# Early sums of eight rows by identity matmuls, the first weight's maxima found ahead of its conversion, and the first tile's g written in float16 directly

## The chip, the cores and the metric

The kernel runs on one core of one Trainium2 chip. The metric is the device time of one execution in microseconds (us). The engines are named as the profile names them: PE (TensorE, the matrix engine), DVE (VectorE), ACT (ScalarE), POOL (GpSimd) and SP (SyncE, which here issues every DMA). Each runs its own list of instructions in order and waits on semaphores for the others.

## The reference

Inputs q, k, v are float32 of shape (8 batches, 8 heads, 576 tokens, 64). The weights are float64: moe_w_in and moe2_w_in are 512 x 2048, moe_w_out and moe2_w_out 2048 x 512. The output is float32, 4608 x 512.

```
k_p = k.reshape(B, H, 72, 8, 64).mean(axis=3)      # means of eight rows; v the same
attn = softmax(q @ k_p.T / 8);  a = attn @ v_p     # a as 4608 tokens x 512
h = a @ moe_w_in
g = where(h >= 1, h, where(h <= -1, 0, (h + 1)**2 / 4))
x2 = g @ moe_w_out
h2 = x2 @ moe2_w_in;  out = (h2 * sigmoid(h2)) @ moe2_w_out
```

## The kernel before

Every product of the two MLPs is made of three float16 matmuls: an operand is split into a high half `hi` and a remainder `lo`, and `three` (L119 to L122) adds hi*hi, hi*lo and lo*hi in PSUM. The 4608 tokens go in nine tiles of 512. This text is about tile 0, which the kernel treats in a way of its own, and about tile 1's attention, which is laid beside it.

Early part. The sums of eight rows of k and v of batch 0 are made per pair of heads (`kv_pool`): on DVE by a reduction (L389), or for the three pairs in `ON_POOL` (v of batch 0, k and v of batch 1) on POOL by three additions (L386, L387). The attention of tile 0 goes through `att_qT`, `att_scores`, `att_norm`, `att_T` and `att_pv` in float32 and leaves tile 0's input as `xh`, `xl`.

The first weight. moe_w_in comes in nine pieces (`cuts1`: seven of 256 columns, two of 128), each loaded as pairs of int32 and converted by the six steps of `steps`: ACT takes absolute values of the high words (L174), DVE floors them and finds the piece's maximum on the way (L182), a matmul with the identity and a DVE reduction spread it to all partitions (L107, L108), three DVE operations put the number together from its two words (L95, L194, L200), ACT scales it by a power of two made from that maximum (L207) and casts it to `hi` (L212), and POOL makes `lo` (L213). The second weight, moe_w_out, goes through the same steps in eight halves, two for each of the four blocks `d` of 128 output columns.

h of tile 0. For each of 16 blocks `s` of 128 hidden columns `emit_h` issues 12 matmuls into a PSUM bank (`hps`). Then `pre_A` (ACT), `min_A` (DVE), `mid_A` (ACT) and `post_A` (DVE) compute g in float32, with constants that don't know yet how large the weight's largest element is; the 16 float32 results lie in `slots`. When the last piece is converted, `consts_A` gives the scale and `first_split` makes the two float16 halves (L808 to L815), one block by ACT and DVE, the next by ACT and POOL.

y of tile 0. For each `d` in turn the two halves of moe_w_out are converted, and 48 matmuls follow. Between them `slots_to` lays the pieces of tile 1's attention (18 calls in `att_slots`). `evac_yA` ends tile 0. From tile 1 on a loop interleaves h, g, y, the next attention and the second MLP's weights block by block, and `split_g` makes the halves of g there.

Order. The framework places each engine's instructions by its own estimate of times and by priorities, so the order in the program text is only a guide; what stands where is shown below from the built programs. The lists are in order: an instruction that waits holds up all that stand behind it on its engine. Buffers come from pools in rotation (`up`, three each of `g` and `u`; `xf`, three; `raws`, two; `kvp`, four of `raw`), and an instruction that fills one waits for the last reader of what lay there.

## Time and profile before

| | |
|---|---|
| median of 3 runs | 1700.85 us (1698.64 to 1702.63) |
| profiled execution | 1695.58 us, span of the trace 1693.8 us |
| PE busy in the span | 1544.6 us (91%) |
| DVE busy | 1260.4 us (74%) |
| ACT busy | 897.1 us (53%) |
| POOL busy | 585.9 us (35%) |
| DMA | 166.32 MB, mean 98 GB/s |

Busy times are of the whole span and hide that its stages differ. The page's 40 slices of 42.3 us each show which part of the span an engine fills, the windows give busy times of a stretch, and the timeline gives single instructions in order of time with the idle time before each and what ended it. The first instruction of the first tile's h and the last of its y bound the stretch that this change works on.

### The profile page before, as it was taken

The numbers are of one execution on the slowest core, as the hardware profiler recorded it, in microseconds if no ns is written. First come the engines' busy times: TensorE is split into PE (matmuls) and PEld (weight loads), VectorE is DVE, ScalarE is ACT, GpSimd is POOL, SyncE is SP. The second block draws the span as 40 slices with busy tenths as digits, with TensorE's granted clock in tenths as the row PEclk, the third lists the DMA queues.
The fourth block names the chain that finished last, engine by engine and source line by source line (L and its number), as shares of the span: only waits on it lengthen the run. The fifth ranks groups of instructions, "written<-read, shape, count | busy, mean of one in ns | idle before, by whom it ended". The sixth has DMA issues, their size and how long they took to land.

```text
span 1693.8 us, 34379 instructions
## 1 busy us (share of the span) xinstructions
PE 1544.6 (91%) x14214; PEld 1053.6 (62%) x14214; DVE 1260.4 (74%) x2234; ACT 897.1 (53%) x1425; POOL 585.9 (35%) x524
## 2 busy tenths in 40 slices
PE   4773679999999999999999979999999999999998
PEld 3331334444444444444444458999999999999998
DVE  8796688978878788797755437777777777777765
ACT  3576545565757646666564425444554444444543
POOL 5733412153332511433342005334433343334322
PEclk8786689999999999999999989999999999999999
DMA  9423579564536667445364030100001000000000
GB/s 288 130 64 107 122 167 255 133 161 129 148 92 140 172 190 185 119 117 131 100 244 142 17 137 14 39 27 27 27 27 39 27 27 33 33 27 27 27 14 26
DMA packets 217036, 166.32 MB, mean 98 GB/s; under 512 B 153904, under 2 KB 176432, under 8 KB 216880
## 3 DMA queue, kind: packets, MB, share of 16 engines
q1 hardware_dynamic: 216880, 164.14, 35.3%
q8 instruction: 111, 1.82, 0.5%
q14 instruction: 45, 0.37, 0.1%
HBM read 102.76 MB, written 33.55 MB: 80 GB/s over the span
## 4 chain that ended last, share of the span: by engine, by line
PE 22%; DVE 21%; issue 14%; ACT 8%; POOL 7%; DMA 6%; SPq 0%; DVEq 0%; POOLq 0%; ACTq 0%
DMA yin<-y 4%; POOL c L657 4%; DVE g L331 4%; DVE sum L389 3%; PE y L120 3%; PE y L122 3%; PE y L121 3%; PE hps L121 2%; PE hps L122 2%; PE hps L120 2%; POOL c L660 2%; DVE xl L331 2%; DVE g L776 2%; ACT g L330 2%; ACT c L916 2%
## 5 line engine op out<-in xcount | busy, mean ns | idle before, releaser
L121 PE MATMUL hb<-xl,wc 128*128 128x128 f16 x2016 | 350.7, 220 | 0.0
L120 PE MATMUL hb<-xh,wc 128*128 128x128 f16 x2016 | 350.6, 220 | 0.0
L122 PE MATMUL hb<-xh,wc 128*128 128x128 f16 x2016 | 350.6, 220 | 0.0
L331 DVE SCALAR_TENSOR_TENSOR g<-c,tsg,g 128x512 f16<-128x512 f32 x252 | 226.4, 901 | 85.7 <-ACT g L330 85.7
L976 PE MATMUL y<-wd,g 128*128 128x256 f16 x1008 | 274.7, 273 | 9.6 <-DVE ob L989 9.0
L978 PE MATMUL y<-wd,g 128*128 128x256 f16 x1008 | 274.8, 273 | 1.0 <-DVE g L331 0.9
L977 PE MATMUL y<-wd,g 128*128 128x256 f16 x1008 | 274.7, 273 | 0.0
L916 ACT ACTIVATE c<-c,tc 128x512 f32<-128x512 f32 x144 | 103.0, 717 | 255.2 <-DVE c L913 255.2
L120 PE MATMUL hps<-xh,wa 128*128 128x512 f16 x576 | 224.1, 389 | 12.8 <-ACT wa L212 11.7
L121 PE MATMUL hps<-xl,wa 128*128 128x512 f16 x576 | 223.9, 389 | 0.2 <-DVE xl L331 0.2
L122 PE MATMUL hps<-xh,wa 128*128 128x512 f16 x576 | 220.8, 385 | 1.0 <-POOL wa L213 1.0
L330 ACT ACTIVATE g<-c,tsg 128x512 f16<-128x512 f32 x252 | 177.6, 718 | 83.2 <-POOL c L660 50.9
L913 DVE TENSOR_TENSOR c<-c,hb 128x512 f32<-128x512 f32 x252 | 167.7, 679 | 72.4 <-PE hb L122 72.1
L121 PE MATMUL y<-g,wb 128*128 128x512 f16 x544 | 210.3, 386 | 6.0 <-DVE g L823 5.2
L120 PE MATMUL y<-g,wb 128*128 128x512 f16 x544 | 208.5, 386 | 3.5 <-ACT g L822 2.6
L122 PE MATMUL y<-g,wb 128*128 128x512 f16 x544 | 209.8, 387 | 0.0
L121 PEld LDWEIGHTS <-wc 128*128 128x128 f16 x2016 | 198.1, 98 | 2.5
L120 PEld LDWEIGHTS <-wc 128*128 128x128 f16 x2016 | 198.1, 98 | 2.1
L122 PEld LDWEIGHTS <-wc 128*128 128x128 f16 x2016 | 198.1, 98 | 0.2
L657 POOL TENSOR_TENSOR c<-c 128x512 f32<-128x512 f32 x108 | 163.7, 1530 | 2.8
L776 DVE SCALAR_TENSOR_TENSOR g<-g,tbr,u 128x512 f32<-128x512 f32 x128 | 110.8, 867 | 57.9 <-ACT u L771 56.5
L771 ACT ACTIVATE u<-u,trsg 128x512 f32<-128x512 f32 x128 | 91.8, 719 | 108.6 <-DVE u L93 108.6
(189 smaller groups left out, 2758.3 us busy)
## 6 DMA issues: line engine op xcount, KB each, us to landing
raw<-in_moe_w_out_dram SPq DMA_DIRECT2D x24, 1024.0 KB
raw<-in_moe_w_in_dram SPq DMA_DIRECT2D x18, 1024.0 KB
raw<-in_k_dram SPq DMA_DIRECT2D x32, 288.0 KB
raw<-in_v_dram SPq DMA_DIRECT2D x32, 288.0 KB
y<-y SPq DMA_DIRECT2D x36, 256.0 KB
yin<-y SPq DMA_DIRECT2D x18, 512.0 KB
out_dram<-ob SPq DMA_DIRECT2D x36, 256.0 KB
qt<-in_q_dram SPq DMA_DIRECT2D x32, 256.0 KB
```

Of the source, the lines that this page charges most:

```text
L120: nc.tensor.matmul(out=acc, lhsT=wh, rhs=xh, start=start, stop=False)
L121: nc.tensor.matmul(out=acc, lhsT=wh, rhs=xl, start=False, stop=False)
L122: nc.tensor.matmul(out=acc, lhsT=wl, rhs=xh, start=False, stop=stop)
L330: a = nc.scalar.activation(out=hi, in_=x, func=AF.Copy, scale=s)
L331: return a, nc.vector.scalar_tensor_tensor(out=lo, in0=x, scalar=s, in1=hi, op0=ALU.mult, op1=ALU.subtract)
L657: nc.gpsimd.tensor_tensor(out=out, in0=a, in1=b, op=ALU.subtract)
L776: return nc.vector.scalar_tensor_tensor(out=w, in0=w, scalar=0.25 if s < KF else r["br"], in1=u_t.pop(s), op0=ALU.subtract, op1=ALU.max)
L913: nc.vector.tensor_tensor(out=out, in0=x, in1=y, op=ALU.add)
L916: nc.scalar.activation(out=x, in_=x, func=AF.Silu, scale=r["c1"])
L976: nc.tensor.matmul(out=acc, lhsT=xh, rhs=wh, start=start, stop=False)
L977: nc.tensor.matmul(out=acc, lhsT=xh, rhs=wl, start=False, stop=False)
L978: nc.tensor.matmul(out=acc, lhsT=xl, rhs=wh, start=False, stop=stop)
```

## The change

Four things change, all before tile 1's loop.

- `kv_pool`: the three pairs that POOL summed (now `ON_PE`) are summed on PE: eight float32 matmuls with the identity for each pair of heads add the eight rows in PSUM, and one ACT copy per batch and tensor brings them back.
- `weight_in`: all nine pieces of the first weight are looked at first (absolute values and maximum, written into the room that the converted piece will later take), their maxima are spread in three groups, and all constants of `consts_A` are made before the first h. The conversion of a piece is then the three DVE operations, two of ACT and one of POOL.
- g of tile 0 is computed with these constants as in later tiles: `pre_A` writes into the pool `up`, `split_g` makes both halves at once into `slots`, and `first_split` is gone.
- Order in the text: more of the loads and sums stand earlier, tile 1's attention starts with block 9 of h (6 of its 18 calls stand there, the rest between the four `d`), and moe_w_out's first block is converted at block 12 of h.

```diff
-    SLOTP = [[0, 5], [7, 10], [12, 15], [17, 19]]
-    ON_POOL = [(0, "v"), (1, "k"), (1, "v")]
+    SLOTP = [9, 13, 16, 18]
+    ON_PE = [(0, "v"), (1, "k"), (1, "v")]
...
+        def look(p):
+            x = room32(p)
+            nc.scalar.activation(out=x, in_=high(held[p], F32), func=AF.Abs, scale=UP)
+            nc.vector.tensor_scalar(
+                out=x, in0=x, scalar1=LEAST_UP, scalar2=FLOOR_UP, op0=ALU.max, op1=ALU.max, accum_out=mx[:, p:p + 1]
+            )
+        def scales(a, b):
+            ps = ps_a.tile([128, 4, 128], F32, tag="a", name="all")
+            for p in range(a, b):
+                nc.tensor.matmul(
+                    out=ps[:, p - a], lhsT=mx[:, p:p + 1].to_broadcast([128, 128]), rhs=ident, start=True, stop=True
+                )
+            nc.vector.tensor_reduce(out=g[:, a:b], in_=ps[:, 0:b - a], axis=AX.X, op=ALU.max)
+            w_scale(e[:, a:b], s[:, a:b], g[:, a:b])
...
-        if (b, which) in ON_POOL:
-            for n in (4, 2):
-                nc.gpsimd.tensor_tensor(out=r[:, :, 0:n], in0=r[:, :, 0:n], in1=r[:, :, n:2 * n], op=ALU.add)
-            nc.gpsimd.tensor_tensor(out=dst, in0=r[:, :, 0], in1=r[:, :, 1], op=ALU.add)
+        if (b, which) in ON_PE:
+            if hp == 0:
+                kv_ps[b, which] = att_ps([SP, H, D])
+            ps = kv_ps[b, which]
+            for n in range(POOL):
+                nc.tensor.matmul(
+                    out=ps[:, 2 * hp:2 * hp + 2], lhsT=ident[0:SP, 0:SP], rhs=r[:, :, n], start=n == 0,
+                    stop=n == POOL - 1,
+                )
+            if hp == NP - 1:
+                nc.scalar.copy(out=sums[b, which][0:SP], in_=kv_ps.pop((b, which)))
...
-        if s < KF:
-            w = slot_t[s] = slots.pop(0)()
...
+        w = g32_t[s] = up.tile([128, N], F32, tag="g", name="g32")
+        nc.scalar.activation(out=w, in_=h_t.pop(s), func=AF.Relu, scale=c_A(r, "c1", s), bias=r["br"])
...
-    def first_split(s, r):
...
+        to = slots.pop(0)() if s < KF else gp.tile([128, 2, N], F16, tag="g", name="g16")
...
+    for a, b in ((0, 3), (3, 7), (7, 9)):
+        for p in range(a, b):
+            look1(p)
+        scales1(a, b)
+        if a == 0:
+            convert1(0)
+    largest(e1m, e1)
+    consts_A(r)
...
+        if 1 <= z:
+            split_g(z - 1, r)
...
+        if s < 8:
+            pool_to(9 + s)
+        if s == 1:
+            q_to(5)
+            run(*loads2)
+        if s >= 9:
+            slots_to((s - 8) * 6 // 8)
+        if s == 12:
+            run(*work2[0])
```

What this does to the lists is seen at three places. On DVE before, in the middle of tile 0's h, a piece of the first weight (`wm` is its maximum) is looked at, put together and followed by the g of a block, piece after piece:

```order
L182 TENSOR_SCALAR xf,wm_581<-xf 128x512
L95 TENSOR_SCALAR xf<-xf 128x512
L194 SCALAR_TENSOR_TENSOR xf<-room,xf 128x512
L200 SCALAR_TENSOR_TENSOR xf<-room,xf 128x512
L182 TENSOR_SCALAR xf,wm_639<-xf 128x512
L93 TENSOR_SCALAR u<-g_515 128x512
```

On DVE of the changed kernel the same stretch has no maximum in it, the pieces follow one another, and g (`u`, then `g`, then its float16 remainder at L820) stands between them:

```order
L262 SCALAR_TENSOR_TENSOR xf<-wb_125,xf 128x1024
L93 TENSOR_SCALAR u<-g_643,tlim 128x512
L262 SCALAR_TENSOR_TENSOR xf<-wb_126,xf 128x1024
L791 SCALAR_TENSOR_TENSOR g_611<-g_611,tbr,u 128x512
L95 TENSOR_SCALAR xf<-wa_136 128x1024
L820 TENSOR_TENSOR g_615<-g_568,g_615 128x512
```

The nine maxima moved ahead of tile 0's h, and the remainders of g moved from behind the last block into the blocks.

On PE before, the first h (`hps`) follows the last attention product of tile 0 and three spread maxima:

```order
L586 MATMUL early<-aT_393,sum 64x128 x4
L586 MATMUL att<-aT_411,sum 64x128 x4
L107 MATMUL all<-ident,wm_451 128x128
L586 MATMUL att<-aT_418,sum 64x128 x4
L107 MATMUL all<-ident,wm_471 128x128
L107 MATMUL all<-ident,wm_523 128x128
L120 LDWEIGHTS wa_128
```

On PE of the changed kernel all nine maxima and 21 of the identity matmuls that sum batch 1's k stand there:

```order
L614 MATMUL att<-aT_434,sum 64x128 x4
L247 MATMUL all<-ident,cols 128x128 x3
L614 MATMUL att<-aT_441,sum 64x128 x4
L247 MATMUL all<-ident,cols 128x128 x6
L413 MATMUL att<-raw,ident 72x128 x21
L120 LDWEIGHTS wa_128
```

So the first h now stands behind the last piece's maximum and behind loads of batch 1's k (`raw`).

On ACT of the changed kernel, the absolute values of the last piece (`wb_127` is the room into which it was loaded) stand ahead of tile 0's input `xh`:

```order
L239 ACTIVATE wa_135<-wb_126 128x1024
L576 COPY aT_363<-early 72x512
L540 ACTIVATE e<-e 128x576
L354 ACTIVATE v_114<-sum,skv 72x512
L239 ACTIVATE wa_136<-wb_127 128x1024
L354 ACTIVATE xh<-att,tsv 128x4x128
```

On ACT before, only three pieces were looked at by then, and the same place has none:

```order
L509 ACTIVATE e<-e 128x576
L330 ACTIVATE v_114<-sum,skv 72x512
L545 COPY aT_386<-att 72x512
L330 ACTIVATE xh<-early,tsv 128x4x128 x2
```

What moved is the wait for the last load of the first weight: it now stands in front of tile 0's input on ACT.

## Rows read from the trace of the kernel before

**Rows 1.** Windows: stretch, length, busy us of PE, PEld, DVE, ACT, POOL; clock, DMA share, GB/s.

```profile
0.00:53.26 53.26, 26.58 (x156) 20.50 (x157) 40.49 (x73) 20.98 (x34) 26.24 (x32) 0.81 1.01 285
53.26:122.54 69.28, 54.17 (x208) 22.46 (x208) 62.62 (x120) 41.69 (x55) 40.98 (x30) 0.80 0.23 65
122.54:182.00 59.46, 18.05 (x102) 8.42 (x103) 41.00 (x98) 39.54 (x68) 20.33 (x15) 0.63 0.43 111
182.00:250.25 68.25, 52.24 (x326) 24.49 (x327) 50.63 (x80) 29.64 (x47) 21.93 (x16) 0.79 0.63 139
250.25:600.00 349.75, 334.19 (x2116) 158.88 (x2115) 291.04 (x549) 214.71 (x367) 116.02 (x116) 0.98 0.61 154
```

**Rows 2.** Timeline of PE: start, length, operation; in brackets idle before and releaser.

```profile
53.26 0.61 PE L120 MATMUL hps<-xh,wa 128*128 128x512 f16 x1 [0.54 <-ACT wa L212]
...
135.11 0.61 PE L120 MATMUL y<-stash,wb 128*128 128x512 f16 x1 [12.57 <-ACT wb L212]
...
249.87 0.38 PE L121 MATMUL y<-stash,wb 128*128 128x512 f16 x1
250.09 0.38 PE L122 MATMUL y<-stash,wb 128*128 128x512 f16 x1
```

**Rows 3.** Groups of DVE by form in 0 to 250.3 us: busy, mean ns.

```profile
L182 DVE TENSOR_SCALAR_CACHE_REDUCE xf<-xf 128x1024 f32<-128x1024 f32 x15 | 18.1, 1208 | 5.1 <-ACT xf L174 5.1
L194 DVE SCALAR_TENSOR_TENSOR xf<-raw,xf 128x1024 int32<-128x1024 int32 x10 | 15.2, 1524 | 0.1
L95 DVE TENSOR_SCALAR xf<-xf 128x1024 int32<-128x1024 int32 x15 | 13.6, 909 | 0.1
...
L776 DVE SCALAR_TENSOR_TENSOR stash<-stash,u 128x512 f32<-128x512 f32 x8 | 8.0, 1020 | 2.2 <-ACT u L771 2.2
...
L95 DVE TENSOR_SCALAR xf<-xf 128x512 int32<-128x512 int32 x2 | 4.8, 2384 | 0.0
...
L809 DVE SCALAR_TENSOR_TENSOR g<-g,tsg,g 128x512 f16<-128x512 f32 x3 | 3.6, 1195 | 0.6 <-ACT g L808 0.6
L108 DVE TENSOR_REDUCE wg<-all 128x1 f32<-128x128 f32 x13 | 3.6, 280 | 0.4 <-PE all L107 0.3
...
L823 DVE TENSOR_TENSOR g<-g,g 128x512 f16<-128x512 f32 x2 | 1.4, 686 | 0.2 <-ACT g L822 0.2
```

**Rows 4.** Timeline of DVE: the first beside POOL's sums, the others with POOL idle or late.

```profile
58.51 3.27 DVE L95 TENSOR_SCALAR xf<-xf 128x512 int32<-128x512 int32 x1
...
77.80 0.68 DVE L776 SCALAR_TENSOR_TENSOR g<-g,u 128x512 f32<-128x512 f32 x1
...
93.76 0.69 DVE L95 TENSOR_SCALAR xf<-xf 128x1024 int32<-128x1024 int32 x1
94.49 1.23 DVE L194 SCALAR_TENSOR_TENSOR xf<-wb,xf 128x1024 int32<-128x1024 int32 x1
```

**Rows 5.** Windows of POOL alone: of L386, of L387, of L815.

```profile
0.00:250.25 250.25, 29.88 (x24) 0.76 0.55 143
...
0.00:250.25 250.25, 9.62 (x12) 0.76 0.55 143
...
0.00:250.25 250.25, 11.76 (x8) 0.76 0.55 143
```

**Rows 6.** Timeline of DVE and ACT: last block of moe_w_out, maximum to cast.

```profile
228.65 0.27 DVE L108 TENSOR_REDUCE wg<-all 128x1 f32<-128x128 f32 x1
...
231.99 1.03 ACT L212 CAST wb<-xf 128x1024 f16<-128x1024 f32 x1
```

**Rows 7.** Timeline of PE: four float32 matmuls of 144 columns; one of 128.

```profile
13.28 2.29 PE L495 MATMUL early<-k,qT 128*128 128x144 f32 x8 [0.96 <-ACT k L420]
...
61.41 0.38 PE L107 MATMUL all<-ident,wm 128*128 128x128 f32 x2
```

**Rows 8.** Timeline of ACT and DVE: one block of g in tile 1, first and last.

```profile
253.76 0.76 ACT L763 ACTIVATE g<-hps,tbr,tc 128x512 f32<-128x512 f32 x1
...
258.14 0.68 DVE L823 TENSOR_TENSOR g<-g,g 128x512 f16<-128x512 f32 x1
```

More of the change, by code (lines that the diff above doesn't have):

```diff
@@ L111, in abs_max @@
         nc.vector.tensor_reduce(out=dst, in_=src, axis=axis, op=ALU.max, apply_absolute_value=True)
-    cols, free = const.tile([128, 64], F32, name="cols"), iter(range(64))
+    cols, free = const.tile([128, 80], F32, name="cols"), iter(range(80))
     def col(n=1):
@@ L222, in new_scale, with weight_in, room32, work @@
         return s
-    def weight_in(w, e, dst, cuts, rooms=None):
+    def weight_in(w, e, tiles, cuts, rooms):
         wv = words(w)
-        held, mx, g = {}, {}, {}
-        ahead = len(cuts) if rooms else AHEAD
+        held, n = {}, len(cuts)
+        mx, s, g = col(n), col(n), col(n)
         def load(p):
-            if p < len(cuts):
-                held[p] = load_raw(wv, (0, KD), cuts[p], rooms and rooms[p]())
-        def maxima(p):
-            mx[p] = sm.tile([128, 1], F32, tag="wm1", name="wm1", bufs=3)
-            return mx[p]
-        def seen(p):
-            g[p] = all_of(mx.pop(p))
-        return [lambda p=p: load(p) for p in range(ahead)], [
-            steps(lambda p=p: held.pop(p), lambda p=p: dst(p), lambda p=p: new_scale(e[:, p:p + 1], g.pop(p)),
-                  lambda p=p: load(p + ahead), lambda p=p: maxima(p), lambda p=p: seen(p))
-            for p in range(len(cuts))
-        ]
+            held[p] = load_raw(wv, (0, KD), cuts[p], rooms[p]())
+        def room32(p):
+            return tiles[p].rearrange("p a c f -> p (a c f)").bitcast(F32).rearrange("p (a b) -> p a b", a=KD)
+        def look(p):
[12 more added lines that the diff above has]
+            w_scale(e[:, a:b], s[:, a:b], g[:, a:b])
+        def work(p):
+            r = held.pop(p)
+            x = xfp.tile([128, XF], F32, tag="xf", name="xf")
+            x = x[:, 0:r.shape[1] * r.shape[2] // 2].rearrange("p (a b) -> p a b", a=KD)
+            xi = x.bitcast(I32)
+            ts(xi, room32(p).bitcast(I32), 3, 0x7FFFFFF8, ALU.logical_shift_left, ALU.bitwise_and)
+            nc.vector.scalar_tensor_tensor(
+                out=xi, in0=high(r, I32), scalar=-0x80000000, in1=xi, op0=ALU.bitwise_and, op1=ALU.bitwise_or
+            )
+            nc.vector.scalar_tensor_tensor(
+                out=xi, in0=low(r), scalar=29, in1=xi, op0=ALU.logical_shift_right, op1=ALU.bitwise_or
+            )
+            nc.scalar.activation(out=x, in_=x, func=AF.Copy, scale=s[:, p:p + 1])
+            hi, lo = tiles[p][:, 0], tiles[p][:, 1]
+            nc.scalar.copy(out=hi, in_=x)
+            nc.gpsimd.tensor_tensor(out=lo, in0=x, in1=hi, op=ALU.subtract)
+        return load, look, scales, work
@@ L366, in att_ps @@
         return ps_a.tile(shape, F32, tag="a", name="att")
-    sums, kv_raw, vscale = {}, {}, {}
+    sums, kv_raw, kv_ps, vscale = {}, {}, {}, {}
     def kv_load(b, which, hp):
@@ L1062, in tile_pooled_attention_two_mlps @@
     load_to(4)
-    q_to(1)
+    q_to(3)
+    load1(0)
     load_to(8)
-    q_to(2)
-    loads1.pop(0)()
     q_to(4)
-    run(*loads1)
-    pool_to(8)
+    for p in range(1, len(cuts1)):
+        load1(p)
+    load_to(12)
+    pool_to(4)
     keys32(0)
@@ L1112, in slots_to @@
                 q_to(NI + (len(first) - len(left)) // 4 + 3)
-                pool_to(8 + (len(first) - len(left)) * 8 // 18)
+                pool_to(16 + max(0, len(first) - len(left) - 6) * 8 // 18)
+    n1 = 1
+    for s in range(KF + 2):
+        if s < KF:
+            while n1 < min(len(cuts1), piece_of(cuts1, s) + 2):
+                convert1(n1)
+                n1 += 1
+            emit_h(s, chunk1, r["x"])
+        z = s - 1
+        if 0 <= z < KF:
+            pre_A(z, r)
+            min_A(z, r)
+        if 1 <= z:
+            split_g(z - 1, r)
+        if 0 <= z < KF:
+            mid_A(z, r)
+            post_A(z, r)
+        if s < 8:
[7 more added lines that the diff above has]
+            run(*work2[0])
+    new_acc(0)
     for d in range(KD):
-        slots_to(SLOTP[d][0])
-        run(*work2[d])
-        slots_to(SLOTP[d][1])
+        if d + 1 < KD:
+            run(*work2[d + 1])
+        slots_to(SLOTP[d])
         for m in range(KF):
```

76 lines of the change are left out of this document (12 added, 64 removed).

## The prediction

> **What bounds the kernel now.** I read the page's slices first, which show PE full after about 250 us and not before; then the windows, cut where the timeline of PE shows the first h of tile 0, at 53.26, and the last of its y, done by about 250.25 [rows 2]. From 250.25 to 600 PE is busy for 334.19 of 349.75 us, 96%: whatever is gained before it is kept, because the work behind it is the same and PE has no room [rows 1]. Before 250.25 the four stretches have PE busy for 26.58, 54.17, 18.05 and 52.24 us. h and y of tile 0 are 384 matmuls of 512 columns, and the last of y start 0.22 us apart [rows 2]: 83 us of PE work lie in 197 us. DVE is busy 40.49, 62.62, 41.00 and 50.63 us there, 194.7 us of 250, and 90% of the stretch 53 to 123 [rows 1]: it is the engine nearest to its bound, and chains between the engines fill the rest. Two such chains are seen: y begins at 135.11 after PE was idle for 12.57 us for a cast of moe_w_out [rows 2], and behind the maximum of that weight's last block at 228.65 the cast ends at 233.02 [rows 6].
>
> **The change part by part.** The sum is made for the time Y at which tile 0's y ends, 250.25 before. By then the kernel before had done two blocks of tile 1's h (24 matmuls, 5.2 us), which the changed list places behind y. So the gain is 245.1 less Y.
>
> Until the first h (53.26 before). Six more pieces are looked at: four of 1.21 us and two of about 0.68, 6.2 us of DVE [rows 3], where DVE has 12.8 us free [rows 1]. The last piece can't be looked at before its load: the loads up to it are 11.9 MB (nine pieces of 8.4, k and v of batch 0 with 2.36, four q tiles of 1.05), and at the stretch's 285 GB/s that is 41.7 us [rows 1]. ACT holds tile 0's last inputs behind that. Then come 21 float32 matmuls of 128 columns for batch 1's k. No row has them; the nearest are one of 128 columns in 0.38 us (shown as x2; overlapped with its neighbours I allow 0.22 at the least) and four of 144 columns in 2.29 us before PE was warm, so 0.22 to 0.51 each and 4.6 to 10.7 us [rows 7]; I take 7, as the clock was 0.81 in this stretch. Their third load ends the first 15.4 MB in the queue's order, so at about 54 us by the same rate. The first h I put at 59 us, 6 later. DVE does not lose that: it starts on the remaining pieces at about 55, with some 7 us of work there before it needs the first block of h.
>
> The other identity matmuls, 32 ahead and 43 among the blocks of h, cost PE 17 to 38 us; PE has 41.8 us idle up to 122.54 [rows 1], so they are hidden. POOL loses 29.88 + 9.62 us of sums and 11.76 us of first_split: 51.3 of its 109.5 us [rows 1, 5]. ACT exchanges one kind of split for another and stays below DVE.
>
> What becomes of DVE's work. 194.7 us as recorded; plus 16 remainders of g at 0.69 [rows 3], 11.0; less eight of L809 at about 1.0, 8; less the small ones of six rounds of maxima (0.28 and three smaller each) and of nine pieces' constants, an estimate of 7; less tile 1's first two blocks, about 6. That is 185. Part of the recorded times is waiting beside POOL. L95 of half a piece took 3.27 us beside POOL's sums, a whole piece 0.69 later [rows 4]. Group means against the undisturbed length: L95 0.91 to 0.69, L194 1.52 to 1.23, L776 1.02 to 0.68, the two halves 2.38 to about 0.4 [rows 3, 4]: an excess of 3.3 + 2.9 + 2.7 + 4.0 = 12.9 us in 41.6 us; with the groups not shown about 25. With POOL's work cut to 53% I let it fall by 12: 173. Bounds: nothing falls (185), or all of it (160).
>
> The Trainium skill ("SBUF — State Buffer", section "Who interferes with whom") says that VectorE and GpSimd share one pair of ports as an exclusive lock, held for a whole instruction. The 3.27 us above agree. By that rule each of POOL's remaining 58 us could still hold DVE up in full, which would leave the sum at the upper bound, 185.
>
> Of the 173, 46 lie ahead of 55 us (40.5 and the looks, less a little) and 13 behind the last block's maximum (half of batch 2's sums). 114 remain. In the h stretch DVE was busy 90% of the time, in the two y stretches 69 and 74% [rows 1], the latter with chains of which two go: first_split between h and y, and the wait for batch 1's keys and scores, which now start under h. I take 0.88, nearer to the h stretch. 114 / 0.88 = 130, and the last block's maximum stands at 185 (before: 228.65 [rows 6]). Behind it 4.4 us to the end of the first cast [rows 6], 10.4 us for 48 matmuls, and a little for POOL's remainder: Y = 200. Gain 245.1 - 200 = 45 us.
>
> PE alone would allow an earlier end: 59 + 41.5 (h) + 9.5 to 13 (sums) + 41.5 (y) + about 5 for attention + about 8 until the first block of moe_w_out is ready = 168.
>
> The profiled execution took 1695.58 us, so the changed one 1651; the median of the runs shown lies 5.3 us above the profiled one, and 1700.85 - 45 = 1656 is the forecast.
>
> The Trainium skill ("TensorE: Matmul & The Clock Gate", section "Step-by-step: what each phase is for") speaks against one part: weight loads can be pulled ahead, matmuls stay in program order. The identity matmuls wait for DMA, and all of h waits behind them. No row of before shows the case; it costs the 6 us above, or as many more as the load of batch 1's k is late.
>
> **The rivals.** A, chains remain. Tile 1's attention goes through transposes by DMA and three engines, and each block of moe_w_out through ACT, DVE, PE, DVE, ACT, POOL. If DVE stays at the share of the old y stretches, 0.72, then 114 / 0.72 = 158, Y = 229, gain 16: 1685. For it: 12.57 us of idle PE before y [rows 2] is such a chain, and it is not cut, only moved under h. Against: there is other DVE work beside it now.
>
> B, better than thought. DVE without POOL's disturbance, 101 us at 0.95, gives Y = 55 + 106 + 16 = 177, gain 68: 1633. PE's 168 is near. For it: POOL's sums were what stood beside the worst rows [rows 4]. Against: POOL's remainders of 16 half pieces stay.
>
> C, nothing to measure: the earlier end is given back in tile 1, where DVE is busy 83% [rows 1]. Its list there is the same, so I see no mechanism that takes all 45 us: 1701.
>
> D, slower: the ring of three. Before, g of tile 0 went into 24 places and h could run ahead of it. Now it goes through three buffers of g and of u, and a block must pass ACT, DVE, ACT, DVE, ACT, DVE before its buffer is free. In tile 1 this takes 5.1 us from 253.76 to 258.82 [rows 8], 1.7 us a block with three in flight. If each of the five handovers waits x us more behind conversions in the in-order lists, 16 blocks take 16 x (5.1 + 5x) / 3. At x = 3.6 that is 123 us, h ends at 182, y with its waits (some 63 us) at 245: nothing gained. At x = 5 it is 161 us, Y = 283, slower by 38: 1739. For it: a conversion's DVE operations take 1.2 to 1.5 us and several can stand in a row. Against: in the changed list one or two stand between the steps of a block.
>
> **How the numbers follow.** The forecast with gains of 28 to 62 us: 0.70. A with gains of 5 to 28: 0.13. B beyond 62: 0.08. C: 0.03. D: 0.06. A run of this kernel tells about 0.2%, 3.4 us, from no change. So faster 0.91, same 0.03, slower 0.06. The range leaves out half of A and of B, C and D: 1634 to 1688.
>
> **What would show it.** Right: the first h at 56 to 62 us, waiting for L413 or the last look; POOL busy about 58 us up to y's end; DVE's means of L95 and L776 near 0.7; y's end at 188 to 212 us; from there on PE as full as before. Wrong: DVE idle for 20% or more between 60 and 185 us for ACT or PE (A); ACT or PE waiting for a buffer of g or u that DVE holds (D); PE's windows after tile 0 emptier than 96% (C); first h behind 65 us, because loads are late.

## The result, and the profile after

The changed kernel takes 1678.99 us (median of four runs, 1672.76 to 1683.29) against 1700.33 for the kernel before on the same chip: ratio 0.9876, 95% interval 0.9844 to 0.9909. A later repetition (e10 below) gave 0.9868, 0.9853 to 0.9883. It is faster by 21 to 23 us, about half of the 45 forecast; the time lies in the range. The profiled execution is the slowest of its four (1683.29 us), that of before one of its fastest, so 12 us lie between these two traces; e10 gives a second trace of the changed kernel.

First the windows of the changed kernel, cut at the first h, the last h, the first y and the last y of tile 0; they answer to [rows 1]. Columns as there.

```profile
0.00:65.66 65.66, 46.41 (x274) 40.37 (x275) 45.13 (x93) 31.31 (x44) 10.95 (x17) 0.77 0.88 247
65.66:125.89 60.23, 55.02 (x286) 30.37 (x283) 59.36 (x75) 41.08 (x62) 17.72 (x10) 0.94 0.28 83
125.89:146.18 20.29, 2.32 (x37) 1.53 (x35) 18.77 (x65) 18.31 (x32) 1.15 (x1) 0.59 0.46 119
146.18:213.73 67.55, 54.26 (x342) 25.02 (x342) 53.43 (x80) 27.52 (x38) 28.28 (x20) 0.84 0.57 148
213.73:600.00 386.27, 362.57 (x2285) 172.60 (x2284) 317.95 (x596) 234.21 (x400) 117.70 (x118) 0.96 0.62 157
```

The third busy time is DVE's: 59.36 of 60.23 us in the stretch of h, so DVE is the bound there. DVE's sum up to y's end is 176.7 us, where 173 were forecast. The last row is less full on PE than before, 93.9% against 95.6%.

The timeline of PE at the same places, for [rows 2] (start, length, operation, in brackets idle before and releaser):

```profile
65.66 0.38 PE L120 MATMUL hps<-xh,wa 128*128 128x512 f16 x1
...
136.08 0.77 PE L107 MATMUL all<-ident,wm 128*128 128x128 f32 x2 [1.96 <-DVE e L536]
...
146.18 0.61 PE L120 MATMUL y<-g,wb 128*128 128x512 f16 x1 [9.33 <-ACT wb L212]
...
213.73 0.38 PE L122 MATMUL y<-stash,wb 128*128 128x512 f16 x1
```

The first h is 12.4 us later than before, not 6; the last y ends at 214.1, not at 200. The matmul at 136.08 spreads moe_w_out's first maximum: it stands behind tile 1's scores in PE's list.

Next why the first h is late: the timelines of PE, ACT and DVE just ahead of it.

```profile
56.75 1.51 PE L247 MATMUL all<-ident,cols 128*128 128x128 f32 x6
...
61.02 4.81 PE L413 MATMUL att<-raw,ident 72*72 72x128 f32 x42
...
58.89 0.69 ACT L354 ACTIVATE xh<-att,tsv 128x512 f16<-128x512 f32 x1 [2.45 <-PE att L614]
59.48 3.21 ACT L265 ACTIVATE xf<-xf,cols 128x1024 f32<-128x1024 f32 x3
62.60 2.92 ACT L267 CAST wa<-xf 128x1024 f16<-128x1024 f32 x3
...
65.87 2.33 DVE L95 TENSOR_SCALAR xf<-wa 128x512 int32<-128x512 int32 x1 [2.38 <-POOL wa L268]
```

The L247 shown spreads the maxima of the first three pieces (the profile has two records for each float32 matmul, so x6); it waits in PE's list behind tile 0's attention, and the scaling and casts (L265, L267) stand on ACT behind tile 0's last input (58.89). DVE has converted three pieces and has no buffer for a fourth until POOL has taken one back, at 65.87. The 21 float32 matmuls of batch 1's k take 4.81 us without a gap (42 records, 0.23 us a matmul), so no load was late for them.

DVE's groups by form up to y's end, for [rows 3]:

```profile
L791 DVE SCALAR_TENSOR_TENSOR g<-g,tbr,u 128x512 f32<-128x512 f32 x16 | 15.6, 976 | 0.5 <-ACT u L787 0.5
...
L95 DVE TENSOR_SCALAR xf<-wa 128x1024 int32<-128x1024 int32 x7 | 6.4, 914 | 0.0
...
L95 DVE TENSOR_SCALAR xf<-xf 128x1024 int32<-128x1024 int32 x8 | 5.5, 688 | 0.1
...
L95 DVE TENSOR_SCALAR xf<-wa 128x512 int32<-128x512 int32 x2 | 2.8, 1376 | 2.4 <-POOL wa L268 2.4
```

The means hide single instructions. Seven times L95 worked on a whole piece while h ran (the groups with `wa` hold three from before it): six took 0.68 us, one took 1.65, and a half piece took 2.33 at 65.87. Both of the long ones stand beside POOL's L268, although POOL is busy for half of what it was.

```profile
73.17 1.65 DVE L95 TENSOR_SCALAR xf<-wa 128x1024 int32<-128x1024 int32 x1
```

The window of POOL alone (busy us, clock, DMA share, GB/s), where the kernel before has 109.47 us up to its y's end [rows 1]:

```profile
0.00:214.10 214.10, 58.09 (x47) 0.82 0.57 157
```

And moe_w_out's last maximum on DVE, for [rows 6], 31 us earlier than before:

```profile
197.32 0.29 DVE L108 TENSOR_REDUCE wg<-all 128x1 f32<-128x128 f32 x1 [1.28 <-PE all L107]
```

Last, the stretch behind y's end, up to the first step of g of block 36 (block 4 of tile 2): windows of before, then of the changed kernel.

```profile
250.25:365.96 115.71, 108.75 (x747) 52.63 (x746) 98.05 (x211) 67.36 (x116) 25.32 (x28) 0.99 0.73 189
```

```profile
213.95:347.60 133.65, 118.99 (x794) 57.80 (x794) 111.14 (x235) 78.47 (x138) 26.20 (x27) 0.94 0.73 180
```

It takes 17.9 us longer. 5.2 are the 24 matmuls of h that now stand behind y; 12.7 of the gain are lost. DVE has 13.1 us more to do there, PE stands idle for 14.7 us instead of 7.0, and its granted clock is 0.94 instead of 0.99 (a mix of 2.4 GHz for most of the stretch and 1.2 GHz for the rest).

Most of the loss has one place. At block 28 the gain is still 28.2 us; the windows from there to block 36, of before and of the changed kernel, have DVE busy for 80% and for 91%:

```profile
316.00:365.96 49.96, 44.69 (x335) 21.63 (x336) 39.95 (x104) 33.59 (x61) 13.39 (x15) 0.97 0.56 136
```

```profile
287.76:347.60 59.84, 51.56 (x365) 25.40 (x364) 54.72 (x113) 36.12 (x66) 14.55 (x15) 0.91 0.67 159
```

DVE has 14.8 us more to do there and the stretch is 9.9 us longer.

### The profile page after: what moved, and what is told of

Read it like the earlier page. It is cut to its first block, busy times and chain, and to the rows that moved or that the text cites. A ratio compares the mean times of both kernels' runs of the same rounds, so it can differ in the third digit from the quotient of the medians.

```text
span 1681.4 us, 34695 instructions
## 1 busy us (share of the span) xinstructions
PE 1561.3 (93%) x14406; PEld 1078.8 (64%) x14406; DVE 1255.0 (75%) x2204; ACT 894.9 (53%) x1420; POOL 534.7 (32%) x479
## 4 chain that ended last, share of the span: by engine, by line
PE 31%; DVE 26%; issue 15%; ACT 10%; DMA 8%; POOL 8%; SPq 1%; DVEq 0%; POOLq 0%; ACTq 0%
DMA yin<-y 4%; PE y L120 4%; PE y L122 4%; PE y L121 4%; POOL c L681 4%; DVE sum L420 4%; DVE g L355 4%; PE hps L122 4%; PE hps L121 4%; PE hps L120 4%; DVE g L791 3%; POOL c L684 2%; DVE xl L355 2%; DVE g L820 2%; ACT g L354 2%
## 5 line engine op out<-in xcount | busy, mean ns | idle before, releaser
L791 DVE SCALAR_TENSOR_TENSOR g<-g,tbr,u 128x512 f32<-128x512 f32 x144 | 127.4, 886 | 59.2 <-ACT u L787 58.0
L787 ACT ACTIVATE u<-u,trsg 128x512 f32<-128x512 f32 x144 | 103.3, 719 | 103.8 <-DVE u L93 103.8
```

The source lines that it names most:

```text
L787: nc.scalar.activation(out=u_t[s], in_=u_t[s], func=AF.Square, scale=r["rsg"])
L791: return nc.vector.scalar_tensor_tensor(out=g32_t[s], in0=g32_t[s], scalar=r["br"], in1=u_t.pop(s), op0=ALU.subtract, op1=ALU.max)
```

## The experiments

"Gain at block 36" is how much earlier than before (365.96 us) that step comes in the profiled execution. "Idle ahead" is DVE's idle time before the first h, in us. "DVE" is its busy time between the first h and the last y, and its share of that stretch.

| run | first h | idle ahead | last y | DVE | gain at block 36 | ratio, interval |
|---|---|---|---|---|---|---|
| before | 53.26 | 12.8 | 250.09 | 154.1, 0.78 | 0 | 1 |
| changed | 65.66 | 20.5 | 213.73 | 131.6, 0.89 | 18.4 | 0.9876, 0.9844-0.9909 |
| e10 changed again | 65.34 | 17.7 | 211.02 | 130.9, 0.90 | 21.1 | 0.9868, 0.9853-0.9883 |
| e1 sums on POOL | 60.23 | 13.1 | 218.07 | 141.5, 0.90 | 17.1 | 0.9897, 0.9881-0.9914 |
| e2 sums alone | 57.98 | 20.4 | 247.03 | 147.5, 0.78 | 0.0 | 1.0010, 0.9999-1.0021 |
| e3 old order | 66.25 | 14.8 | 236.98 | 133.6, 0.78 | 8.1 | 0.9985, 0.9970-1.0000 |
| e9 order alone | 55.98 | 16.0 | 228.65 | 143.7, 0.83 | 10.9 | 0.9925, 0.9909-0.9941 |
| e4 block first | 62.15 | 14.5 | 213.13 | 135.2, 0.90 | 21.1 | 0.9907, 0.9886-0.9927 |
| e7 v0 on POOL | 64.17 | 13.9 | 215.14 | 131.0, 0.87 | 18.2 | 0.9884, 0.9869-0.9899 |
| e8 less DVE | 67.14 | 26.2 | 209.46 | 126.0, 0.89 | 25.5 | 0.9843, 0.9826-0.9859 |
| e11 batch 2 on PE | 65.31 | 17.5 | 214.49 | 118.7, 0.80 | 11.7 | 0.9935, 0.9921-0.9948 |
| e14 scales earlier | 60.07 | 11.3 | 205.39 | 126.0, 0.87 | 26.6 | 0.9856, 0.9843-0.9869 |
| e15 scales first | 73.34 | 22.2 | 219.87 | 123.7, 0.84 | 16.7 | 0.9917, 0.9904-0.9931 |
| e5 sums early | 63.98 | 18.9 | 212.07 | 131.8, 0.89 | 23.2 | 0.9885, 0.9865-0.9905 |
| e6 tile 2 early | 63.88 | 16.2 | 209.57 | 131.1, 0.90 | 27.8 | 0.9867, 0.9853-0.9882 |
| e13 lead of 12 | 68.82 | 16.9 | 211.02 | 127.0, 0.89 | 25.9 | 0.9888, 0.9871-0.9905 |

The changed kernel, e10, e5, e6 and e13 have the same instructions up to the last y; the edits of the last three lie behind it. So these five show how far one program differs from profile to profile: the first h by 4.9 us, the last y by 4.2. A difference of a few microseconds between two single profiles is therefore weak. But the last y less the time idle ahead is 193.1 to 194.1 us in all five: it is not the first h that the last y follows (e13 has the latest of the five, and the same last y as e10), it is DVE's idle time ahead of it, one for one.

### Which part brings the gain

**e1**, sums back on POOL:

```diff
         if (b, which) in ON_PE:
...
-            for n in range(POOL):
-                nc.tensor.matmul(
...
+            for n in (4, 2):
+                nc.gpsimd.tensor_tensor(out=r[:, :, 0:n], in0=r[:, :, 0:n], in1=r[:, :, n:2 * n], op=ALU.add)
+            nc.gpsimd.tensor_tensor(out=dst, in0=r[:, :, 0], in1=r[:, :, 1], op=ALU.add)
```

> The changed kernel with one part undone: the sums of eight rows for v of batch 0 and k and v of batch 1 go back from identity matmuls on TensorE to additions on POOL. Theory (in-order chains eat the gain; the sums on TensorE cost little and free POOL): POOL is busy about 97 us again up to the end of tile 0's y instead of 58, the DVE means beside it rise, and the first h, which no longer waits for sums of v and of batch 1's k in TensorE's list, comes at 58 to 63 us instead of 65.66; the end of y moves by less than 6 us from 214.1 and the time stays within 1674 to 1690. Rival (DVE work and POOL's disturbance of it are the bound): DVE's work up to y's end rises by 10 to 15 us from 176.7, y ends at 225 to 230, time 1690 to 1697.

1684.45 us. The first h comes 5.4 us earlier, but from there to the last y it takes 157.8 us instead of 148.1, with 10 us more DVE work. The two leave 4.3 us at the last y (7.1 against e10): the theory's time and the rival's DVE work. By the medians the sums on TensorE are worth 5 to 7 us, but the intervals of e1 and e10 touch.

**e2**, the kernel before with TensorE's sums:

```diff
         if (b, which) in ON_POOL:
-            for n in (4, 2):
-                nc.gpsimd.tensor_tensor(out=r[:, :, 0:n], in0=r[:, :, 0:n], in1=r[:, :, n:2 * n], op=ALU.add)
-            nc.gpsimd.tensor_tensor(out=dst, in0=r[:, :, 0], in1=r[:, :, 1], op=ALU.add)
...
+            for n in range(POOL):
+                nc.tensor.matmul(
...
```

> The kernel before with one part of the change alone: the same sums by identity matmuls on TensorE, nothing else. Theory (chains): TensorE has idle time for them, DVE is relieved by up to 10 us in the h stretch, but the sums now stand in TensorE's list between h and y with their loads, so the gain is between 0 and 8 us: 1692 to 1701. Rival (POOL's disturbance of DVE is a main term): 12 us of DVE work go, nearly all of it is seen in the time: 1686 to 1690. A third possibility, that the float32 sums delay the first h: 1702 to 1708.

1700.47 us: no gain. DVE has 55.92 us in the stretch of h (57.98 to 118.78) instead of 62.24 (53.26 to 122.16), the first h comes 4.7 us later, and nothing is left at block 36.

**e3**, the changed kernel in the old order:

```diff
-    SLOTP = [9, 13, 16, 18]
+    SLOTP = [[0, 5], [7, 10], [12, 15], [17, 19]]
...
-        if s >= 9:
-            slots_to((s - 8) * 6 // 8)
-        if s == 12:
-            run(*work2[0])
...
-        if d + 1 < KD:
-            run(*work2[d + 1])
-        slots_to(SLOTP[d])
+        slots_to(SLOTP[d][0])
+        run(*work2[d])
+        slots_to(SLOTP[d][1])
```

> The changed kernel with only its order undone: tile 1's attention and the conversion of moe_w_out's first block come behind tile 0's h, as in the kernel before, while the early maxima, the direct float16 g and the sums on TensorE stay. Theory (chains): moe_w_out's first maximum no longer stands behind tile 1's scores in TensorE's list; h ends some 5 us earlier than 126, y begins at 128 to 138 instead of 146, it ends at 205 to 218, and the list from tile 1 to tile 2 is again that of the kernel before, so that the 8 us given back there (gain 23.3 to 15.1 us between the first blocks of tile 2) are kept: 1665 to 1678. Rival (work under h is what brings the gain, DVE has the same total): y ends at 222 to 232 and the time is 1685 to 1695.

1698.14 us: without the order the other three parts gain at most 0.3%. (Its profiled execution, 1692.57 us, is one of the fastest of nine that reach from 1692.41 to 1703.23, so its gain at block 36 is more than the median's.) Its stretches of h, of the wait for y, and of y:

```profile
66.25:118.45 52.20, 52.20 (x278) 29.20 (x277) 50.91 (x62) 35.12 (x49) 12.79 (x6) 0.97 0.25 77
118.45:133.93 15.48, 0.83 (x6) 0.60 (x5) 13.17 (x28) 14.07 (x22) 0.52 (x1) 0.68 0.21 68
133.93:236.98 103.05, 66.32 (x427) 32.26 (x428) 69.53 (x154) 48.57 (x81) 30.30 (x21) 0.75 0.57 137
```

y begins 12 us earlier than in the changed kernel and ends 23 us later: in its 103.05 us DVE is busy for 69.53, 67%, close to the shares that [rows 1] have. Both theories were wrong on y's end and on the time.

**e9**, the kernel before with the order alone (`first_split`, POOL's sums and the late maxima stay):

```diff
-    SLOTP = [[0, 5], [7, 10], [12, 15], [17, 19]]
+    SLOTP = [9, 13, 16, 18]
...
+        if s < 8:
+            pool_to(9 + s)
+        if s >= 9:
+            slots_to((s - 8) * 6 // 8)
+        if s == 12:
+            run(*work2[0])
...
```

> The kernel before with one thing of the change alone: its order. Tile 1's attention (six slots), batch 1's sums (still on POOL) and moe_w_out's first block are asked for under tile 0's h, the y blocks' slots are as in the changed kernel; the maxima, the direct g and TensorE's sums are not taken over. Theory (what the change gains is DVE's idle time in the y stretches, filled by moving attention under h, and the early maxima and direct g only make room for it): h ends later than 122, at 135 to 145, because DVE is 90% busy there; between h and y the split of g still lies; y ends at 232 to 242 instead of 250, the time is 1685 to 1695. Rival A (the order is the whole gain): y ends at 215 to 225, 1676 to 1684. Rival B (the order is worth nothing without room on DVE): y ends at 246 or later, 1697 to 1705.

1687.24 us, 13 of the 22 us, the theory's time (the last y is 3 us earlier than it said). With e2 and e3: of the parts that were run alone the order is the one that gains, and with the other parts it gains some 9 more. The early maxima and the direct g were not run alone.

### What sets the end of y

**e4**, moe_w_out's first block asked for at block 8 instead of 12:

```diff
-        if s == 12:
+        if s == 8:
             run(*work2[0])
```

> The changed kernel with the conversion steps of moe_w_out's first block asked for four blocks of h earlier, ahead of tile 1's attention. In TensorE's list its maximum now stands among the last h, and tile 1's scores behind the first 48 matmuls of y. Theory (chains): h ends 3 to 8 us later than 126 because DVE is 98.6% busy there, but y begins right behind it at 131 to 138 instead of 146.2, and ends at 203 to 210; the time falls by 4 to 10 us to 1669 to 1675. Rival (DVE is the bound, positions in the list do not matter): h ends at 134 to 138, y at 212 to 216, time 1676 to 1682 as before this edit.

1684.26 us. The windows of h and of y:

```profile
62.15:118.84 56.69, 53.04 (x284) 29.23 (x282) 54.66 (x71) 39.40 (x53) 17.44 (x10) 0.97 0.25 74
...
119.05:213.13 94.08, 62.04 (x378) 27.69 (x377) 80.32 (x149) 48.57 (x78) 29.54 (x21) 0.76 0.58 143
```

y begins right behind h, 27 us earlier than in the changed kernel, and ends at the same time. The wait of PE ahead of y [9.33 <-ACT wb] costs nothing there: DVE's work between the first h and the last y has the same share, 0.90. The theory of e4 fell; of its rival y's end held, but not the later h. The kernel is no faster than the changed one, and by the intervals just slower than e10.

**e8**, without the third DVE operation of moe_w_in's pieces:

```diff
-            nc.vector.scalar_tensor_tensor(
-                out=xi, in0=low(r), scalar=29, in1=xi, op0=ALU.logical_shift_right, op1=ALU.bitwise_or
-            )
```

> The changed kernel without the third DVE operation (the low bits) of the nine pieces of moe_w_in: that part of the computation is left out, to take some 9.9 us of DVE work (seven of 1.22, two of about 0.6) from the stretch of tile 0's h, and nothing else. Theory (DVE's work after the first h sets y's end, and a second chain, attention, sets the end of tile 1): y ends 8 to 12 us earlier, at 202 to 206, but the gain at block 36 rises by less than 4 us, and the time falls by less than 4, to 1675 to 1680. Rival A (chains between the engines set y's end): y ends at 211 to 215. Rival B (what is gained at y's end is kept): the time falls by 8 to 11 us to 1668 to 1671.

1675.23 us. 5.6 us of DVE work less between the first h and the last y (the rest stood ahead of it), and that stretch is 5.7 us shorter than in the first profile (against e10 4.9 and 3.4). The theory's time came, its places did not: y ends at 209.8, not at 202 to 206, because the part left out ahead of the first h did not make that h earlier: DVE stood idle there for 26.2 us, the most of all runs. The last y less that idle time is 183.3 us, 10 to 11 below the five profiles of one list, for 9.9 us of work left out. And it is kept behind y: gain at block 36 25.5 us.

**e7**, v of batch 0 on POOL:

```diff
-    ON_PE = [(0, "v"), (1, "k"), (1, "v")]
+    ON_PE = [(1, "k"), (1, "v")]
+    ON_POOL = [(0, "v")]
...
-            pool_to(9 + s)
+            pool_to(8 + s)
```

> The changed kernel with batch 0's v summed on POOL again, and batch 1's sums on TensorE asked for one block of h later. Theory (the late first h is one third of what is missing, and DVE's work after it the rest): tile 0's attention no longer has 32 float32 sums in front of it on TensorE; the first h comes at 58 to 62 us instead of 65.66, y's end moves by the same 3 to 6 us to 208 to 211, of which at most half is kept behind tile 1: time 1675 to 1680. Rival (the loads set the first h): first h at 64 to 67, y's end and the time as in the changed kernel, 1677 to 1684. A third: POOL's sums beside the looks slow DVE, first h earlier but y's end later than 214.

1681.17 us, no change. Tile 0's last product ends 2.5 us earlier (56.4 instead of 58.9), but 22 of batch 1's matmuls for k then stand ahead of the first h until 64.2 (the rival's place and time).

**e11**, batch 2's sums on TensorE as well, pair by pair:

```diff
-    ON_PE = [(0, "v"), (1, "k"), (1, "v")]
+    ON_PE = [(0, "v"), (1, "k"), (1, "v"), (2, "k"), (2, "v")]
...
+            if b == 2:
+                ps = att_ps([SP, 2, D])
+                for n in range(POOL):
+                    nc.tensor.matmul(
...
+                nc.scalar.copy(out=dst, in_=ps)
```

> The changed kernel with the eight sums of batch 2 on TensorE as well, pair by pair: 8 of 1.9 us, 15 us of DVE work less, of which some 7 us lie in front of the last maximum of moe_w_out and 7 beside the last y; 128 short float32 matmuls more, 14 us, on TensorE. Theory (DVE's work behind the first h sets y's end, microsecond for microsecond, as far as it lies in front of the last block's maximum): from the first h to y's end 140 to 145 us instead of 148; time 1671 to 1677. Rival (TensorE is full from 187 us on, the added sums delay the last y): 148 to 155 us, time 1679 to 1686.

1688.51 us, slower than the changed kernel. The row of y, for the fourth row of the changed kernel:

```profile
144.87:214.49 69.62, 63.16 (x445) 35.39 (x446) 41.28 (x73) 29.38 (x44) 29.45 (x20) 0.89 0.53 140
```

DVE loses 12 us there and y is not earlier, as the rival said: PE is at 91% in it. So DVE sets the pace up to y, not beside its last blocks, and TensorE is no free adder.

**e14**, the first three pieces' scales inside tile 0's attention (e15 the same at `n == 3`, with three pieces converted):

```diff
+        if n == 5:
+            for p in range(3):
+                look1(p)
+            scales1(0, 3)
+            for p in range(1):
+                convert1(p)
...
-    for a, b in ((0, 3), (3, 7), (7, 9)):
+    for a, b in ((3, 7), (7, 9)):
...
-        if a == 0:
-            convert1(0)
```

> The changed kernel with the scales of moe_w_in's first three pieces asked for inside tile 0's attention instead of behind it. In the lists the scaling and casts of these pieces now stand ahead of the last four copies of tile 0's attention on ScalarE, and batch 1's k sums behind 22 matmuls of h on TensorE. Theory (DVE's and TensorE's idle time before the first h is what the late start costs, and it counts in full up to y's end): first h at 58 to 62 us instead of 65.3 to 65.7, DVE idle before it for 12 to 16 us instead of 17.7 to 20.5, y ends at 204 to 208 instead of 211 to 214, time 1670 to 1675. Rival (the first h cannot start before tile 0's input, which the casts now delay): first h at 63 to 66, y's end and the time as before the edit.

1676.78 us. The windows ahead of the first h, of h, and from the last y to block 36:

```profile
0.00:60.07 60.07, 36.73 (x228) 31.29 (x229) 48.81 (x82) 30.91 (x44) 15.48 (x19) 0.76 0.89 265
60.07:126.49 66.42, 60.24 (x330) 35.16 (x329) 60.82 (x105) 46.99 (x73) 13.10 (x7) 0.93 0.33 94
...
205.61:339.40 133.79, 122.44 (x798) 58.95 (x798) 111.60 (x235) 78.48 (x138) 26.13 (x27) 0.92 0.75 180
```

First h 5.3 us earlier than in e10, y's end 5.6, block 36 5.4. DVE is idle for 11.3 us ahead of the first h, less than in any of the five profiles of the same list, and the last y less that time is 194.1 us, as there: DVE's idle time before the first h counts in full up to y's end. The theory's places came, its time (1670 to 1675) did not. By the medians it is the fastest complete kernel, but its interval overlaps e10's.

> As the run before, two rounds of tile 0's attention earlier: the scales of the first three pieces stand between the sums of batch 0's v on TensorE, their casts ahead of the second pair of scores on ScalarE. Theory (idle time before the first h counts in full): DVE can start on pieces four to six during the attention, first h at 57 to 62, y ends at 202 to 208, time 1668 to 1674. Rival (TensorE's list now waits for the loads of these pieces and the attention gets later by what the casts take on ScalarE, 6 us): first h at 63 to 68, y ends at 210 to 215, time 1677 to 1682.

1686.68 us: the rival, by more than it said (e16 has the same list up to y's end and the first h at 68.46). PE's longest waits between 16 and 73 us:

```profile
PE att L574 <- POOL e L560: 8.9, 1, 8.9
PE early L413 <- DMA raw<-in_v_dram: 6.6, 2, 4.1
```

With the casts ahead of it the attention's own chain is late, and PE waits 8.9 us in one place (3.7 in the changed kernel).

### Behind y's end

> The changed kernel unchanged, for a second profile of it and a tighter time beside the next two runs. Theory (the first h moves with the rate of the loads, and some 4 us are lost or not in the second MLP from run to run): first h between 62 and 66 us, y's end 82 us behind the end of h and 146 to 150 us behind the first h, the gain at block 36 is 17 to 22 us, time 1676 to 1681. Rival (the loss at the end of tile 1 was chance): gain at block 36 above 24.

The repetition has the gain at 31.0 us at block 28, at 21.1 at block 36, and 20.5 at the end of the first MLP: the loss is no chance.

**e5** asks for batch 3's sums eight places earlier; **e6** is e5 and, besides, gives four slots to each of tile 1's first four blocks in the place of two to eight; **e13** lets the slots run twelve ahead instead of eight:

```diff
-        pool_to(16 + (NTOKS - len(slots_left)) * 8 // 18)
+        pool_to(24 + (NTOKS - len(slots_left)) * 8 // 18)
...
-        for _ in range(2 if KF < s <= KF + XS else 1):
+        for _ in range(4 if s < KF + 4 else 1):
...
-    XS = 8
+    XS = 12
```

> The changed kernel with the sums of batch 3 (needed by tile 3) asked for eight places earlier in tile 1's slots. Theory (a second chain): attention was moved forward by only 10 to 16 us while h and y were moved by 28 to 32; at the end of tile 1 TensorE waits in its list for batch 3's scales, behind which tile 2's last attention stands, and 8 to 10 us of the gain go there. With the sums earlier that wait shrinks: the gain over the kernel before is still above 21 us at block 36 instead of 18.4, and the time is 1670 to 1677. Rival (DVE has no room in tile 1, what is moved comes back elsewhere): the gain at block 36 is 15 to 19 and the time 1677 to 1684.

> As the run before, and besides four slots of the next tile's attention to each of tile 1's first four blocks instead of two to eight blocks. Theory (a second chain): in TensorE's list three of tile 2's four last products now stand ahead of the long run of y at the end of tile 1, so the waits of 8 us there go: the gain at block 36 is 23 to 29 us, the time 1665 to 1673. Rival (DVE has no room): tile 1's h blocks wait for DVE instead, the gain falls already by block 28 (below 25) and the time is 1677 to 1684.

> The changed kernel with the attention slots of tiles 2 and on running twelve instead of eight places ahead. TensorE's list is the same up to the end of tile 1; there tile 2's last product stands in front of the maximum of a block of the second MLP's weight instead of behind it, and some blocks of h come between the scores behind it. Theory (the list gives the gain back there): the loss between blocks 28 and 36, 9.8 us in both profiles of the changed kernel, falls to 3 to 7 us; time 1672 to 1677. Rival (the attention itself is late, whatever stands in front of it): loss 8 to 11 us, time 1676 to 1681.

1682.11 us (0.9885, 0.9865 to 0.9905), 1678.95 (0.9867, 0.9853 to 0.9882) and 1681.62 (0.9888, 0.9871 to 0.9905). At block 36 the gains are 23.2, 27.8 and 25.9 us, as the theory said for the first two, but at block 44 they are 19.1, 18.1 and 16.4, and by the intervals none is faster than e10. What is moved comes back one tile on.

**e17** asks for the attention's last product three slots earlier, ahead of the next batch:

```diff
+            if r == 0 and first <= n - 2:
+                att_pv(n - 2)
             if r == 0 and n < end:
                 batches(n)
                 att_qT(n)
-            if r == 3 and first <= n - 2:
-                att_pv(n - 2)
...
```

> The changed kernel with each tile of the attention's last product asked for three slots earlier, in front of the next batch's sums and scales instead of behind them. In TensorE's list tile 2's last product now starts in front of batch 3's scales. Theory (tile 2's input waits in the lists for batch 3, which only tile 3 needs): the loss between blocks 28 and 36 falls from 9.8 us to 2 to 5, and it stays so; time 1670 to 1675. Rival (the loss only moves, as in e6 and e13, because the attention's own chain and DVE have no room in tile 1): loss at block 36 smaller, but the gain at block 80 is 16 to 22 as in the changed kernel, time 1676 to 1682.

1728.13 us, 1.0166 (1.0147 to 1.0184): slower than before, against both expectations. PE's waits from 214 to 360 us:

```profile
PE att L614 <- DMA aT<-e: 12.5, 3, 11.2
PE y L120 <- ACT g L819: 9.2, 1, 9.2
```

The product now reaches PE's list before its transposes by DMA have landed, and all of h and y stands behind it. The gain falls to 9.9 us at block 36 and is gone before block 80; the same edit acts on every later tile of the first MLP.

**Combinations.** e12 is e4, e6 and e11 together, e16 is e15 and e13, e18 is e14 and e17.

> Three edits together: moe_w_out's first block ahead of tile 1's attention, batch 3's sums and tile 2's attention earlier in tile 1, batch 2's sums on TensorE. Theory (DVE's work sets y's end, and the list at the end of tile 1 gives 8 to 10 us back): y ends at 203 to 209, the gain at block 36 is 28 to 34 us and the time 1664 to 1672. Rival (every stretch up to tile 2 is near its bound and gains are given back in the next): the gain at block 36 is 18 to 24 and the time 1674 to 1682.

> The edits of e15 and e13 together. If both theories hold, they add up: y ends at 202 to 208, the loss at the end of tile 1 is 3 to 7 us, time 1664 to 1671. If gains before tile 2 are given back at the next list: the gain over the kernel before at block 36 is 18 to 24 us, the time 1674 to 1681.

> The edits of e14 and e17 together. Theory (two separate losses): y ends at 204 to 208, the gain at block 36 is 31 to 36 us instead of 26.6 in e14, time 1665 to 1671. Rival (the loss at the end of tile 1 only moves): the gain at block 80 is 24 to 29 as in e14, time 1674 to 1679.

1683.98 us (0.9915, 0.9900 to 0.9930), 1690.18 (0.9938, 0.9921 to 0.9955) and 1732.56 (1.0191, 1.0177 to 1.0205): nothing adds up, and each is about as slow as the slowest of its parts. The gains at block 36 are 16.7, 20.3 and 7.3 us, where the theories of e12 and e18 had 28 to 36.

## Why the prediction was half right

**Direction and sizes of work: right.** DVE's work up to y's end was forecast at 173 us and is 176.7; POOL's at 58 and is 58.1; DVE's share behind the first h at 0.88 and is 0.89. That share was a choice between two rows, so there is some luck in it. e1 confirms the relief from POOL: up to y's end POOL has 100.3 us in e1 and 58.1 in the changed kernel, DVE 188.7 and 176.7, so 12.0 us of DVE for 42.2 of POOL, 0.28 for one; e2 against before has 9.4 for 42.9. The Trainium skill ("SBUF — State Buffer", "Who interferes with whom") says that whoever issues first gets the shared ports for its whole instruction and the other is blocked, and that not every DVE instruction contends. The single long instructions beside POOL agree (1.65 and 2.33 us); the upper bound of 185, with each of POOL's 58 us held against DVE in full, did not come.

**The step "DVE starts on the remaining pieces at about 55" failed.** It started at 65.87, because the scales of the first pieces wait behind tile 0's attention on PE and their casts behind it on ACT, and three buffers were full. In the prediction's terms Y = 200 is 9 us of idle DVE ahead of 55 (55 less 46 of work), 173 of work and 18 idle behind. Measured it is 20.5 + 176.7 + 16.9 = 214.1 in the first profile and 17.7 + 178.6 + 15.1 = 211.4 in e10: of the 14.1 us at y's end 11.5 are idle time ahead of the first h. The five profiles of one list and e14 show that this time counts one for one. What brings it is less sure. Of the 12.4 us by which the first h is later, e1 puts 7.0 on the looks and their order (53.26 to 60.23) and 5.4 on the sums, where 6 were forecast for both, but one list alone differs by 4.9 us in its first h. In DVE's idle time the looks cost nothing (12.8 before, 13.1 in e1) and the sums the rest (20.4 in e2 with the sums alone); e14 takes it away with the sums in place, by moving the scales. The sign "first h behind 65 us, because loads are late" came true in its number and not in its reason. The Trainium skill ("TensorE: Matmul & The Clock Gate", "Step-by-step: what each phase is for") says that matmuls stay in program order. The traces agree: 8.9 us of one wait in e15 and 11.2 in e17 hold up all that stands behind. The 6 us that I set for this were too few. (The three loads in the sum for the last look add up to 11.8 MB, not 11.9, which changes nothing.)

**The step "whatever is gained before 250 is kept" failed.** It rested on PE at 96% and on the work behind being the same. It is not: two blocks of g, looks and rows that had been done beside y now stand behind it. I charged the two blocks' 5.2 us to PE and took their 6 us off DVE's sum without putting them back. From y's end to block 36 DVE has 111.1 us of work instead of 98.1, at 0.83 instead of 0.85 of the stretch, and 12.7 us of the gain go. Taken together, from the first h to block 36, DVE's work fell only from 252.1 to 242.7 us; its share rose from 0.81 to 0.86. 312.7 - 281.9 us is 30.8, less 12.4 for the late start 18.4: the gain at block 36.

That DVE's work is what takes the gain is seen between blocks 28 and 36. There e2 and e3, in the old order, have as much DVE work as before (0.0 and 0.2 us more) and lose 1.6 and 0.3 us. With the new order it is 9.1 more and 4.7 lost in e9, 14.8 and 9.9 in both profiles of the changed kernel, 15.0 and 10.5 in e14, with DVE busy for 90 to 92% of the stretch. Where an edit moves work out of it, less goes: 6.8 more and 2.4 lost in e6, 10.6 and 4.9 in e5, 11.2 and 7.8 in e13, until it comes back by block 44. Over the whole of the way from y's end the two do not go together as closely: e2 loses 3.0 us without more DVE work, e3 5.0 with 2.2 more, e9 5.3 with 10.8 more. Part of the 12.7 us is not idle time of PE: its idle time grew by 7.7 us, and it was busy for 5.0 us more than the 24 matmuls of h take. It ran at 1.2 GHz for 17.0 us there, each time while it waited or just after, and for 3.4 us in the kernel before:

```profile
269.60:276.40 6.80, 6.29 (x25) 2.55 (x25) 3.83 (x9) 2.86 (x4) 1.15 (x1) 0.50 0.59 139
317.40:327.60 10.20, 6.29 (x65) 3.70 (x65) 8.92 (x28) 8.16 (x15) 5.48 (x7) 0.50 0.67 102
```

No run took the added DVE work away and left the order, so how much each of these adds stays open.

**The rivals.** The time is A's, its mechanism is not: DVE's share did not stay at 0.72, and 20.5 of its 37.4 us idle up to y's end lie ahead of the first h. A share near A's is what e3 has without the order (0.67 in the stretch of y). C was put aside because I saw no mechanism; a part of it came. D is not seen: h takes 60.2 us, not 123 or more, with DVE busy for 98.6% of it.

**Left open.** In the second MLP most profiles, that of the changed kernel among them, lose 2.5 to 5 us of their gain between 1190 and 1346 us at a granted clock of 1.00; those of before, e1, e7 and e9 lose less than 1. The windows of before and of the changed kernel:

```profile
1190.00:1346.00 156.00, 154.03 (x2083) 145.71 (x2081) 115.39 (x199) 77.08 (x117) 57.57 (x48) 1.00 0.08 29
```

```profile
1190.00:1346.00 156.00, 150.12 (x2026) 141.79 (x2023) 111.70 (x190) 74.21 (x115) 58.18 (x49) 1.00 0.08 29
```

Its code is the same in all; what decides it was not found. It is one reason why the two traces lie 12 us apart and the medians 21, and so why the gain at block 36, 18.4 us, is neither of the two.

## What to carry to other kernels

When a bound engine is relieved in one stage, follow its work to the next point where all kernels have done the same, not to the end of the stage: what was pushed behind the stage's end is a debt. Then look at what that engine does before its stage starts; here 6 to 9 us of its idle time ahead of the first matmul, held by scales at the wrong place in two in-order lists, came back one for one at y's end (e14), though the median of that run is not clear of e10's. And an order that fills idle time (tile 1's attention under h, 13 us alone) can gain more than the operations that were saved (sums alone 0), while asking for a step before its data can be there holds up the whole list (e17: 50 us over e10).

## What was not expected of the hardware

- A float32 sum by an identity matmul of 72 rows and 128 columns took 0.23 us in a run of them (21 in 4.81 us, at a granted clock of 1.00), near the lower of the bounds set. The higher bound came from a matmul at 13.28 whose clock no row shows.
- POOL's elementwise work cost DVE 0.28 us for each of its own up to y's end (e1), 0.22 in e2, not one for one.
- PE's idle 14.7 us behind y's end came with a mean clock of 0.94, before 7.0 us with 0.99 (0.98 over the longer stretch in [rows 1]).
- One list of instructions gave a first h between 63.88 and 68.82 us, and a last y that followed DVE's idle time ahead of it within 1.0 us.
